# Attention into a token-and-channel mixer: the key maximum's broadcast and the key-value product moved beside h1, with the broadcast multiplied by the identity

## Chip, cores and metric

The kernel runs on one core of one Trainium2 chip. The metric is the device time of one execution in microseconds (us). Before the change it is 837.05 us, the median of 3 runs (833.13 to 837.97).

## What is computed

For 8 samples with 8 heads of 576 positions by 64 channels, both softmaxes (of q along its channels, of k along the positions) feed a linear attention, and its output `x` (576 x 512 for each sample) goes through a mixer along the positions and one along the channels. Cut to what matters:

```python
q_s = softmax(q, axis=-1)          # maximum taken off, exp, sum + 1e-9
k_s = softmax(k, axis=2)           # along the positions
kv  = einsum('bhsd,bhse->bhde', k_s, v)
x   = einsum('bhsd,bhde->bhse', q_s, kv)         # as (b, 576, 512)
h   = relu(x.T @ w_tok1) @ w_tok2                # along the positions, 576 -> 256 -> 576
u   = x + h.T
out = u + relu(u @ w_ch1) @ w_ch2                # along the channels, 512 -> 1536 -> 512
```

The weights come as float64 and are brought to float32 on the chip.

## The kernel before, in words

A *unit* is one pair of heads of one sample: 128 channels by 576 positions (five blocks of 128, the last one half filled). There are 32 units, four to a sample (j = 0 to 3). Units 0 to 7 ("early") are worked off ahead of the large loop, units 8 to 31 ("late") inside it.

A unit's stages, with the lines of the profile:

- `load_unit` (L123) issues the loads of kt (L128), q (L131) and, for late units, k (L135) on the SP queue; `load_v` (L141) those of v (L145, L146). For late units there is one buffer for kt and one for v, and there are two each for q and k.
- `softmax_k` (L205): VectorE takes the maximum `mc` of each channel from kt, which has the channels on its partitions (L208). k has them along its free dimension, so for a late unit the maximum has to be laid along the free dimension on all partitions: ScalarE writes the identity scaled by `mc` into `dg` (L223), TensorE multiplies a tile of ones by it (L225, "the broadcast" below), ScalarE copies the result to `mb` (L227), GpSimd subtracts it from k (L228), ScalarE takes the exponential (L229).
- `softmax_q` (L231): VectorE and ScalarE (L236 to L242); for a late unit q is then split into a high part `qh` (ScalarE) and a low part `ql` (GpSimd, both L105/L106), as are nearly all operands of the large products.
- `stage_qT` (L278): VectorE turns q in blocks of 32 (L297), 16 copies on VectorE and ScalarE put the blocks in place (L305), and q is split again into `qth`, `qtl`.
- `stage_kv` (L252): ten matmuls (L259, two column tiles of 64, one for each head; 20 records, since an unsplit float32 matmul is recorded as two), VectorE's reciprocal of the sum (L264, L265), ScalarE's scaling into `kvf` (L269), the split into `kvh`, `kvl`.
- `stage_y` (L308): 14 split matmuls of 256 columns (L319) and a copy `ys` (L321).
- `stage_h1` (L324): two unsplit matmuls of 128 columns (L327, four records), then `hh` on ScalarE (L334) and `hl` on VectorE (L335).
- `stage_u` (L346), two halves: nine split matmuls each (L364), of `kvh`/`kvl` with `qth`/`qtl` and of `hh`/`hl` with w_tok2, then a split of the result into the slot `uT` (L371, L372).

The large loop has 108 steps: 9 groups g of 512 positions by 12 blocks f. A step is `ch1(g, f)` (L385: 12 split matmuls of 512 columns, L393, then `h2h` on ScalarE L396 and `h2l` on VectorE L397) and then `ch2` (L401, 12 matmuls of 512 columns, L406) of the step before it. At the end of a group `out_end` (L423) adds the residual to the four accumulators (L430) and issues the output's DMAs; `residual` (L414) computes that residual ahead on GpSimd (L419) into staging tiles, which the output's DMAs of the group before must have left.

The work of the late units is put between: the dictionary `todo` holds functions for the place after ch1 of step i (key i) and after ch2 of step i (key i + 0.5). For a unit of the samples 3 to 7, whose steps start at `n0 + (b - 3) * 12`, n0 = 24:

```python
at = [n0 + (b - 3) * NF + 3 * j + x for x in (0, 1, 1.5, 2)]
...
put(at[0], s1)                          # stage_qT, stage_kv of unit n
put(at[0], lambda n=n: soft(n + 1))     # softmax_k, softmax_q of unit n + 1
put(at[0] + 0.5, lambda n=n: begin(n + 2))
```

and then stage_y at the second place, stage_h1 and the first half of stage_u together at the third, the other half at the fourth. So the unit with j = 0 has stage_kv and the next unit's broadcast in the first step of a group.

This order is not the engines' order yet. A planner in the framework simulates the program with costs of its own and, on each engine, takes among the instructions that its simulation has ready the one that stands first in the program. An engine's queue then runs in the order so found. All small products of the units and ch1 share four PSUM banks (`ps_h`); ch2's accumulators hold the other four.

Of the kernel before, what the change touches and what calls it, by code (L numbers as in the profile page):

```python
# [8 lines left out]
F32 = mybir.dt.float32  # L9
F32R = mybir.dt.float32r  # L10
U32 = mybir.dt.uint32
AF = mybir.ActivationFunctionType
ALU = mybir.AluOpType
AX = mybir.AxisListType

P = 128
# [4 lines left out]
def attn_mixer_kernel(ctx: ExitStack, tc: tile.TileContext, q, k, kt, v, wt, out, dims):  # L21
# [3 lines left out]
    nc = tc.nc  # L25
    B, H, S, D, TOK, DM, DCH, wide = dims
    NJ = DM // P
    NF = DCH // P
    NT = TOK // P
    C = S // P  # L30
    C1 = C + 1
    S0 = C * P
    TL = S - S0
    NG = B * S // CW
    NU = B * NJ
    NE = 2 * NJ
    F_HEAD, F_MORE = 4, 8

    const = ctx.enter_context(tc.tile_pool(name="const", bufs=1))
# [3 lines left out]
    sm = ctx.enter_context(tc.tile_pool(name="sm", bufs=2))  # L43
# [7 lines left out]
    ident = const.tile([P, P], F32R, name="ident")  # L51
# [3 lines left out]
    def v_tile(pool):  # L55
        t = pool.tile([P, C1, 2, D + 1], F32, name="v_t")
        nc.gpsimd.memset(t[:, :, :, D : D + 1], 1.0)
        nc.gpsimd.memset(t[TL:P, C, :, :], 0.0)
        return t

    v_ring = [v_tile(const)]

    ones = const.tile([P, P], F32, name="ones")
    nc.gpsimd.memset(ones, 1.0)


    ebias = const.tile([P, 1], F32, name="ebias")
    nc.gpsimd.memset(ebias, -(896.0 + 20.0) * 2.0**23)
# [1 line left out]
    def kv_tile(pool, i):  # L70

        t = pool.tile([P, P], F32, name=f"kvf{i}")
        nc.gpsimd.memset(t, 0.0)
        return t

    kv_ring = [kv_tile(const, 0)]

    w1h = const.tile([P, C, TOK], F32R, name="w1h")
    w1l = const.tile([P, C, TOK], F32R, name="w1l")
# [20 lines left out]
    def f32(ap):  # L100
        return ap.bitcast(F32)

    def split(hi, lo, src, lo_eng):

        nc.scalar.copy(hi, src)  # L105
        lo_eng.tensor_tensor(lo, src, f32(hi), op=ALU.subtract)  # L106
# [3 lines left out]
    def ps_unit(dtype=F32):  # L110

        pools = unit_banks[0]
        pool, name = pools[turn[0] % len(pools)]
        turn[0] += 1
        return pool.tile([P, 512], dtype, name=name)
# [25 lines left out]
    def load_v(n):  # L141
        if n < NU and n not in v_of:
            t = v_ring[n % 2 if n < NE else 0]
            for h in range(2):
                nc.sync.dma_start(t[:, 0:C, h, 0:D], v[n][:, 0:C, h * D : (h + 1) * D])  # L145
            nc.sync.dma_start(t[0:TL, C, :, 0:D], v[n][0:TL, C, :].rearrange("p (h d) -> p h d", h=2))  # L146
            v_of[n] = t
# [54 lines left out]
        split(*c2[f], load_weights(AT_C2 + f), nc.vector)  # L202


    def softmax_k(u):  # L205
        ktt = u["kt"]
        mc = sm.tile([P, 1], F32, name="mc")
        nc.vector.tensor_reduce(mc, ktt, axis=AX.X, op=ALU.max)  # L208
        kx = u["k"]
        if u["early"]:  # L210
            nc.vector.tensor_scalar(mc, mc, -1.0, None, op0=ALU.mult)
            nc.scalar.activation(ktt, ktt, AF.Exp, bias=mc)
            t = ps_unit()
            for c in range(C):
                nc.tensor.transpose(t[:, c * P : (c + 1) * P], ktt[:, c * P : (c + 1) * P], f32(ident))
            nc.scalar.copy(kx[:, 0:C, :], t.rearrange("p (c d) -> p c d", c=C))
            t = ps_unit()
            nc.tensor.transpose(t[:, 0:P], ktt[:, S0 : S0 + P], f32(ident))
            nc.scalar.copy(kx[:, C, :], t[:, 0:P])
            return  # L220

        dg = sm.tile([P, P], F32, name="dg", bufs=1)
        nc.scalar.activation(dg, f32(ident), AF.Copy, scale=mc)  # L223
        t = ps_unit()
        nc.tensor.matmul(t[:, 0:P], ones, dg, start=True, stop=True)  # L225
        mb = sm.tile([P, P], F32, name="mb", bufs=1)
        nc.scalar.copy(mb, t[:, 0:P])  # L227
        nc.gpsimd.tensor_tensor(kx, kx, mb.unsqueeze(1).broadcast_to([P, C1, P]), op=ALU.subtract)  # L228
        nc.scalar.activation(kx, kx, AF.Exp)  # L229
# [22 lines left out]
    def stage_kv(u):  # L252
        kx, vt = u["k"], v_of[u["n"]]
        kv = ps_unit()

        for c in range(C1):
            for h in range(2):
                hs = slice(h * D, (h + 1) * D)
                nc.tensor.matmul(kv[hs, 0 : D + 1], kx[:, c, hs], vt[:, c, h, :], start=(c == 0), stop=(c == C))  # L259

        if u["n"] != NE - 1:
            load_v(u["n"] + 2 if u["n"] < NE else u["n"] + 1)
        rs = sm.tile([P, 1], F32, name="rs")
        nc.vector.tensor_scalar(rs, kv[:, D : D + 1], 1e-9, None, op0=ALU.add)  # L264
        nc.vector.reciprocal(rs, rs)  # L265
        kvf = kv_ring[u["n"] % len(kv_ring)]
        for h in range(2):
            hs = slice(h * D, (h + 1) * D)
            nc.scalar.activation(kvf[hs, hs], kv[hs, 0:D], AF.Copy, scale=rs[hs])  # L269
        u["kvf"] = kvf  # L270
        if u["early"]:
            return
        kvh = wk.tile([P, P], F32R, name="kvh")
        kvl = wk.tile([P, P], F32R, name="kvl")
        split(kvh, kvl, kvf, nc.vector)
        u["kvh"], u["kvl"] = kvh, kvl
# [68 lines left out]
    def stage_u(u, half):  # L345
        b, j = u["b"], u["j"]  # L346
        edge = (b + 1) * CW - b * S
        cut = min(max(edge, S - 320), 320)
        n0, n1 = ((0, cut), (cut, S))[half]
        N = n1 - n0  # L350
        ns = slice(n0, n1)
        t = ps_unit()
        if u["early"]:
            mm = [(u["kvf"], u["qt"][:, ns])]
        else:
            mm = [(u["kvh"], u["qth"][:, ns]), (u["kvh"], u["qtl"][:, ns]), (u["kvl"], u["qth"][:, ns])]
        for n in range(NT):
            mm += [
                (u["hh"][:, n, :], w2h[:, n, ns]),
                (u["hh"][:, n, :], w2l[:, n, ns]),  # L360
                (u["hl"][:, n, :], w2h[:, n, ns]),
            ]
        for i, (a, w) in enumerate(mm):
            nc.tensor.matmul(t[:, 0:N], a, w, start=(i == 0), stop=(i == len(mm) - 1))  # L364
        for g, a0, a1 in ((b, n0, min(n1, edge)), (b + 1, max(n0, edge), n1)):
            if a0 < a1:
                at = b * S + a0 - g * CW
                uh, ul = (x[:, j, at : at + a1 - a0] for x in uT[g])
                src = t[:, a0 - n0 : a1 - n0]
                emptied[:] = [  # L370
                    nc.scalar.copy(uh, src).ins,  # L371
                    nc.vector.tensor_tensor(ul, src, f32(uh), op=ALU.subtract).ins,  # L372
                ]
# [68 lines left out]
    units = {}  # L442

    def begin(n):
        if n < NU and n not in units:
            units[n] = load_unit(n // NJ, n % NJ)

    def soft(n):
        if n < NU:
            softmax_k(units[n])  # L450
            softmax_q(units[n])

    def pe_stages(n):
        def s1():
            stage_qT(units[n])
            stage_kv(units[n])

        def s2():
            stage_y(units[n])

        def s3():
            stage_h1(units[n])
            stage_u(units[n], 0)

        def s4():
            stage_u(units[n], 1)

        return s1, s2, s3, s4


    NB = 3
    early_pools = ExitStack()
    early = early_pools.enter_context(tc.tile_pool(name="early", bufs=NB))
    early1 = early_pools.enter_context(tc.tile_pool(name="early1", bufs=1))
# [2 lines left out]
    w1f = early1.tile([P, C1, TOK], F32, name="w1f")  # L477
    w1t = early1.tile([P, TOK], F32, name="w1t")
    v_ring.append(v_tile(early1))
    kv_ring += [kv_tile(early1, i) for i in range(1, NB)]  # L480


    stages = [pe_stages(n) for n in range(NE)]
# [22 lines left out]
            with behind(emptied):  # L506
                split_tok1()
    early_pools.close()
    del v_ring[1:], kv_ring[1:]
    ld = ctx.enter_context(tc.tile_pool(name="ld", bufs=2))  # L510
    wk = ctx.enter_context(tc.tile_pool(name="wk", bufs=1))
    c2_rows(F_HEAD, F_MORE)
# [8 lines left out]
    n0 = len(steps)  # L521
    steps += [(g, f) for g in range(2, NG) for f in range(NF)]

    todo = {}

    def prepare():
        begin(NE)
        begin(NE + 1)
        soft(NE)

    def put(at, fn):
        todo.setdefault(int(2 * at) / 2, []).append(fn)

    put(n0 - 12, prepare)
    for n in range(NE, NU):
        b, j = divmod(n, NJ)
        if b == 2:
            at = (n0 - 10, n0 - 9, n0 - 9, n0 - 7.5) if j == 0 else [n0 - 9.5 + 2 * j + x for x in (0, 0.5, 1, 1.5)]
        else:
            at = [n0 + (b - 3) * NF + 3 * j + x for x in (0, 1, 1.5, 2)]  # L540
        s1, s2, s3, s4 = pe_stages(n)
        put(at[0], s1)
        put(at[0], lambda n=n: soft(n + 1))
        put(at[0] + 0.5, lambda n=n: begin(n + 2))
        for x, fn in zip(at[1:], (s2, s3, s4)):
            put(x, fn)

    pend = None

# [84 lines left out]
```

## Time and profile before

| what | before |
|---|---|
| median of 3 runs | 837.05 us |
| runs | 837.05, 833.13, 837.97 us |
| profiled execution | 836.64 us, of which its span (first to last instruction) is 834.8 us |
| mean granted TensorE clock | 0.994 |
| instructions | 11727 |
| busy | TensorE 807.8 us (97%), VectorE 492.6 us (59%), ScalarE 321.2 us (38%), GpSimd 113.3 us (14%) |
| DMA | 63.54 MB, mean 76 GB/s |

In a view of groups a row is: line, engine, operation, output<-inputs, shapes, count | busy us, mean ns of one | idle time before them and who ended it. In a timeline a row is: start in us, length in us, engine, line, operation, output<-inputs, shapes, count, and in brackets the idle time just before it with who ended it. The lengths of matmuls overlap, because they are pipelined; the distance between two starts is what a matmul costs in a stream.

### The profile page before, as it was taken

What the parts mean: (1) busy time and instruction counts of PE and PEld (TensorE: products, weight loads), DVE (VectorE), ACT (ScalarE), POOL (GpSimd) and SP (SyncE); (2) the same over time, 40 slices, a digit from 0 to 9 for tenths busy, and PEclk for the clock granted to TensorE, in tenths of its full rate; (3) what the DMA queues carried; (4) which work ended last, traced back from release to release, by engine and by line L of the source; (5) the groups of instructions that cost most, each with busy time, mean ns of one, the idle gap of its engine ahead of it and who ended that gap; (6) DMA issues with size and microseconds to landing.
All of it is one profiled execution on the core that took longest, in us unless ns stands there. A gap on an engine that the chain in (4) does not pass through costs nothing.

```text
span 834.8 us, 11727 instructions
## 1 busy us (share of the span) xinstructions
PE 807.8 (97%) x4464; PEld 673.8 (81%) x4464; DVE 492.6 (59%) x1088; ACT 321.2 (38%) x746; POOL 113.3 (14%) x93
## 2 busy tenths in 40 slices
PE   3899999989999999999999999999999999999997
PEld 3788888778888888788888888888888888888885
DVE  7999989899775555755556555755565323112111
ACT  4676443455544334433434433434443321101110
POOL 1000000112211011311122011311131102002000
PEclk9999999999999999999999999999999999999999
DMA  8653532424222122322232221312121001001001
GB/s 272 184 165 108 190 130 84 131 75 135 76 66 79 54 54 62 97 62 62 62 113 62 62 62 42 95 54 62 42 85 47 15 1 51 1 0 51 1 1 51
DMA packets 60632, 63.54 MB, mean 76 GB/s; under 512 B 40864, under 2 KB 40992, under 8 KB 60576
## 3 DMA queue, kind: packets, MB, share of 16 engines
q1 hardware_dynamic: 55392, 53.36, 21.9%
q10 hardware_dynamic: 5184, 9.44, 3.0%
q8 instruction: 35, 0.57, 0.3%
q14 instruction: 21, 0.17, 0.1%
HBM read 53.35 MB, written 9.44 MB: 75 GB/s over the span
## 4 chain that ended last, share of the span: by engine, by line
PE 79%; DVE 12%; DMA 4%; issue 2%; ACT 1%; POOL 1%; SPq 0%; DVEq 0%; POOLq 0%; ACTq 0%
PE ps_h L393 31%; PE ps_o L406 31%; PE ps_h L364 6%; PE ps_h L319 4%; DVE q_t L305 3%; PE ps_h L259 2%; DMA out<-stg 2%; DMA q_t<-in_q 1%; PE ps_h L327 1%; PE ps_o L364 1%; PE ps_h L225 1%; DVE q_t L237 1%; DMA stg<-in_w 1%; DVE st L236 1%; POOL ql L106 1%
## 5 line engine op out<-in xcount | busy, mean ns | idle before, releaser
L397 DVE SCALAR_TENSOR_TENSOR h2l<-ps_h,h2h 128x512 fp32r<-128x512 f32 x108 | 74.1, 686 | 173.6 <-ACT h2h L396 173.6
L393 PE MATMUL ps_h<-uh,c1h 128*128 128x512 f32 x432 | 171.8, 398 | 0.0
L393 PE MATMUL ps_h<-ul,c1h 128*128 128x512 f32 x432 | 171.5, 397 | 0.0
L393 PE MATMUL ps_h<-uh,c1l 128*128 128x512 f32 x432 | 171.3, 396 | 0.0
L406 PE MATMUL ps_o<-h2h,c2l 128*128 128x512 f32 x432 | 169.1, 392 | 0.0
L406 PE MATMUL ps_o<-h2h,c2h 128*128 128x512 f32 x432 | 168.4, 394 | 0.2 <-ACT h2h L396 0.2
L396 ACT ACTIVATE h2h<-ps_h 128x512 fp32r<-128x512 f32 x108 | 64.4, 596 | 261.8 <-PE ps_h L393 255.7
L406 PE MATMUL ps_o<-h2l,c2h 128*128 128x512 f32 x432 | 152.4, 396 | 0.0
L305 DVE COPY q_t<-cv_s 32x160 f32<-32x160 f32 (+1 forms) x264 | 71.7, 272 | 62.5 <-POOL ql L106 59.2
L393 PEld LDWEIGHTS ps_h<-ul,c1h 128*128 128x128 f32 x432 | 81.8, 189 | 19.4
L393 PEld LDWEIGHTS ps_h<-uh,c1l 128*128 128x128 f32 x432 | 81.7, 189 | 17.0
L393 PEld LDWEIGHTS ps_h<-uh,c1h 128*128 128x128 f32 x432 | 81.6, 189 | 17.1
L406 PEld LDWEIGHTS ps_o<-h2h,c2h 128*128 128x128 f32 x432 | 81.1, 188 | 17.3 <-ACT h2h L396 0.4
L406 PEld LDWEIGHTS ps_o<-h2h,c2l 128*128 128x128 f32 x432 | 81.2, 188 | 16.9
L406 PEld LDWEIGHTS ps_o<-h2l,c2h 128*128 128x128 f32 x432 | 79.6, 188 | 16.3
L228 POOL TENSOR_TENSOR k_t<-k_t,mb 128x640 f32<-128x640 f32 x24 | 37.7, 1572 | 324.6 <-ACT mb L227 324.6
L106 POOL TENSOR_TENSOR ql<-q_t,qh 128x640 fp32r<-128x640 f32 x24 | 38.2, 1592 | 189.5 <-DMA stg<-in_w 100.7
L419 POOL TENSOR_TENSOR stg<-uh,ul 128x512 f32<-128x512 f32 x28 | 35.5, 1290 | 144.5 <-DMA out<-stg 86.8
L236 DVE TENSOR_REDUCE st<-q_t 128x10 f32<-128x640 f32 x32 | 26.1, 817 | 37.2 <-DMA q_t<-in_q 37.2
L238 ACT ACTIVATE q_t<-q_t 128x640 f32<-128x640 f32 x32 | 23.7, 741 | 45.3 <-DVE q_t L237 45.1
L305 ACT COPY q_t<-cv_s 32x128 f32<-32x128 f32 (+1 forms) x120 | 36.8, 307 | 2.2 <-DVE cv_s L297 0.8
L364 PE MATMUL ps_h<-w2h,hh 128*128 128x256 f32 (+1 forms) x112 | 32.9, 301 | 0.0
(143 smaller groups left out, 1150.4 us busy)
## 6 DMA issues: line engine op xcount, KB each, us to landing
stg<-in_w SPq DMA_DIRECT2D x28, 512.0 KB, 4.1
kt_t<-in_kt SPq DMA_DIRECT2D x32, 320.0 KB, 3.4
q_t<-in_q SPq DMA_DIRECT2D x32, 320.0 KB, 3.0
v_t<-in_v SPq DMA_DIRECT2D x64, 128.0 KB, 2.9
out<-stg ACTq DMA_DIRECT2D x32, 256.0 KB, 2.8
k_t<-in_k SPq DMA_DIRECT2D x24, 320.0 KB, 3.6
v_t<-in_v SPq DMA_DIRECT2D x32, 32.0 KB, 3.1
out<-part ACTq DMA_DIRECT2D x4, 256.0 KB, 2.7
```

What stands on the lines that cost most here:

```text
L106: lo_eng.tensor_tensor(lo, src, f32(hi), op=ALU.subtract)
L228: nc.gpsimd.tensor_tensor(kx, kx, mb.unsqueeze(1).broadcast_to([P, C1, P]), op=ALU.subtract)
L236: nc.vector.tensor_reduce(st[:, 0, :], qt, axis=AX.X, op=ALU.max)
L238: nc.scalar.activation(qc, qc, AF.Exp)
L305: eng(qx[ys, 0:n, xs], turned[xs, 0:n, ys])
L319: nc.tensor.matmul(y[:, 0:TOK], a, w, start=(i == 0), stop=(i == len(mm) - 1))
L364: nc.tensor.matmul(t[:, 0:N], a, w, start=(i == 0), stop=(i == len(mm) - 1))
L393: nc.tensor.matmul(t, a[:, f, n, :], w, start=(i == 0), stop=(i == 3 * NJ - 1))
L396: nc.scalar.activation(hh, t, AF.Relu).ins,
L397: nc.vector.scalar_tensor_tensor(hl, t, 0.0, f32(hh), op0=ALU.max, op1=ALU.subtract).ins,
L406: nc.tensor.matmul(o, a[:, cs], w, start=(first and i == 0), stop=(last and i == 2))
L419: nc.gpsimd.tensor_tensor(res[n], f32(uh), f32(ul), op=ALU.add)
```

## The change

The late units' stages are no longer kept together by unit. `softmax_k` is divided into `k_max` (the maximum) and `exp_k` (broadcast, subtraction, exponential); `stage_kv` loses its last lines to `split_kv`. In the broadcast the stationary operand is now the maximum itself, read with a stride of zero, and the moving one the identity; `dg` and `ones` are gone. Two of the three small tiles `kvf` live for the whole kernel instead of one, so that kv of a unit can be written while the unit before still has its own.

```diff
-    ones = const.tile([P, P], F32, name="ones")
-    nc.gpsimd.memset(ones, 1.0)
...
-    kv_ring = [kv_tile(const, 0)]
+    kv_ring = [kv_tile(const, i) for i in range(2)]
...
+    def exp_k(u):
+
         kx = u["k"]
...
-        dg = sm.tile([P, P], F32, name="dg", bufs=1)
-        nc.scalar.activation(dg, f32(ident), AF.Copy, scale=mc)
         t = ps_unit()
-        nc.tensor.matmul(t[:, 0:P], ones, dg, start=True, stop=True)
+        nc.tensor.matmul(t[:, 0:P], u["mc"].broadcast_to([P, P]), f32(ident), start=True, stop=True)
...
-    kv_ring += [kv_tile(early1, i) for i in range(1, NB)]
+    kv_ring.append(kv_tile(early1, 2))
...
-    del v_ring[1:], kv_ring[1:]
+    del v_ring[1:], kv_ring[2:]
...
+    at = [n0 - 8.5 + 2 * j for j in range(NJ)]
+    at += [n0 + (b - 3) * NF + 3 * j + 1 for b in range(3, B) for j in range(NJ)]
+    load(10, NE)
+    load(10, NE + 1)
+    put(11, k_max, NE)
+    put(11, exp_k, NE)
+    put(11, softmax_q, NE)
+    put(13, k_max, NE + 1)
+    put(13.5, exp_k, NE + 1)
+    put(13.5, stage_kv, NE)
+    put(14, split_kv, NE)
+    put(14, stage_qT, NE)
+    put(15, stage_y, NE)
+    put(15, softmax_q, NE + 1)
+    for i, a in enumerate(at):
+        n = NE + i
+        load(a - 1, n + 2)
+        put(a - 0.5, k_max, n + 2)
+        put(a, stage_h1, n)
+        put(a, exp_k, n + 2)
+        put(a, stage_kv, n + 1)
+        put(a + 0.5, lambda u: stage_u(u, 0), n)
+        put(a + 1, lambda u: stage_u(u, 1), n)
+        put(a + 1, split_kv, n + 1)
+        put(a + 1, stage_qT, n + 1)
+        if n + 1 < NU:
+            put(at[i + 1] - (1 if at[i + 1] - a > 2 else 0.5), stage_y, n + 1)
+            put(at[i + 1] - (1 if at[i + 1] - a > 2 else 0.5), softmax_q, n + 2)
```

So at a place `a` (steps 1, 4, 7 and 10 of a group, from sample 3 on) there stand h1 of unit n, the broadcast of unit n + 2 and kv of unit n + 1; the halves of stage_u follow half a step and a whole step later, stage_y stands a whole step ahead of h1 instead of half a step.

More of the change, by code (lines that the diff above doesn't have):

```diff
@@ L202, in load_ch, with k_max @@
         split(*c2[f], load_weights(AT_C2 + f), nc.vector)
+    def k_max(u):
+        mc = sm.tile([P, 1], F32, name="mc")
+        nc.vector.tensor_reduce(mc, u["kt"], axis=AX.X, op=ALU.max)
+        u["mc"] = mc
     def softmax_k(u):
-        ktt = u["kt"]
-        mc = sm.tile([P, 1], F32, name="mc")
-        nc.vector.tensor_reduce(mc, ktt, axis=AX.X, op=ALU.max)
-        kx = u["k"]
[L210 to L220, printed above, removed]
-        dg = sm.tile([P, P], F32, name="dg", bufs=1)
-        nc.scalar.activation(dg, f32(ident), AF.Copy, scale=mc)
+        k_max(u)
+        ktt, mc, kx = u["kt"], u["mc"], u["k"]
+        nc.vector.tensor_scalar(mc, mc, -1.0, None, op0=ALU.mult)
+        nc.scalar.activation(ktt, ktt, AF.Exp, bias=mc)
+        t = ps_unit()
+        for c in range(C):
+            nc.tensor.transpose(t[:, c * P : (c + 1) * P], ktt[:, c * P : (c + 1) * P], f32(ident))
+        nc.scalar.copy(kx[:, 0:C, :], t.rearrange("p (c d) -> p c d", c=C))
+        t = ps_unit()
+        nc.tensor.transpose(t[:, 0:P], ktt[:, S0 : S0 + P], f32(ident))
+        nc.scalar.copy(kx[:, C, :], t[:, 0:P])
+    def exp_k(u):
+        kx = u["k"]
         t = ps_unit()
-        nc.tensor.matmul(t[:, 0:P], ones, dg, start=True, stop=True)
+        nc.tensor.matmul(t[:, 0:P], u["mc"].broadcast_to([P, P]), f32(ident), start=True, stop=True)
         mb = sm.tile([P, P], F32, name="mb", bufs=1)
@@ L266, in stage_kv @@
         kvf = kv_ring[u["n"] % len(kv_ring)]
+        u["kvf"] = kvf
         for h in range(2):
@@ L269, in stage_kv, with split_kv @@
             nc.scalar.activation(kvf[hs, hs], kv[hs, 0:D], AF.Copy, scale=rs[hs])
-        u["kvf"] = kvf
-        if u["early"]:
-            return
+    def split_kv(u):
+        kvf = u["kvf"]
         kvh = wk.tile([P, P], F32R, name="kvh")
@@ L524, in attn_mixer_kernel, with put, load @@
     todo = {}
[L526 to L546, printed above, removed]
+    def put(at, fn, n):
+        if n < NU:
+            todo.setdefault(int(2 * at) / 2, []).append(lambda: fn(units[n]))
+    def load(at, n):
+        if n < NU:
+            todo.setdefault(int(2 * at) / 2, []).append(lambda: begin(n))
+    at = [n0 - 8.5 + 2 * j for j in range(NJ)]
[26 more added lines that the diff above has]
+            put(at[i + 1] - (1 if at[i + 1] - a > 2 else 0.5), softmax_q, n + 2)
     pend = None
```

## The prediction

> **What bounds the kernel now.** I read the page first: busy time by engine, then the chain that ended last; then the busy time by stretch; then the waits of TensorE (PE); then PE's timeline at the places that the change touches.
>
> ```profile
> PE 807.8 (97%) x4464; PEld 673.8 (81%) x4464; DVE 492.6 (59%) x1088; ACT 321.2 (38%) x746; POOL 113.3 (14%) x93
> ...
> PE 79%; DVE 12%; DMA 4%; issue 2%; ACT 1%; POOL 1%; SPq 0%; DVEq 0%; POOLq 0%; ACTq 0%
> ```
> ```profile
> 140.00:240.00 100.00, 97.52 (x545) 81.75 (x544) 86.93 (x186) 49.77 (x115) 19.37 (x13) 0.98 0.31 95
> 240.00:690.00 450.00, 447.80 (x2585) 375.50 (x2584) 251.45 (x582) 178.09 (x434) 79.54 (x54) 1.00 0.21 61
> ```
>
> From 240 to 690 us, where 20 of the 24 late units are worked off, PE is busy 447.8 of 450 us. VectorE (DVE) has nearly half its time free there, ScalarE (ACT) and GpSimd (POOL) more. After 690 no unit is left and nothing of the change reaches. From 140 to 240 DVE is at 87 of 100 us and close to being the bound. So time is won in one way only: PE has to do less, or wait less. "Busy" hides part of that, as records of matmuls overlap; what a piece costs PE is read from the distance between starts. The waits that the profile names for PE in the stretches touched are few, one at the start of the late units (its row stands below) and four of this kind:
>
> ```profile
> PE ps_h L364 <- DVE hl L335: 2.2, 4, 0.9
> ```
>
> **The change part by part.**
>
> *Standing together.* The words of the change suggest that small unsplit matmuls are dear because each interrupts the stream of split ones. What does such an interruption cost? First h1 and the broadcast alone:
>
> ```profile
> 171.74 0.39 PE L406 MATMUL ps_o<-h2l,c2h 128*128 128x512 f32 x1
> 171.97 0.60 PE L327 MATMUL ps_h<-kvf,ys 128*128 128x128 f32 x4
> ```
> ```profile
> 204.12 0.39 PE L406 MATMUL ps_o<-h2h,c2l 128*128 128x512 f32 x1
> 204.35 0.38 PE L225 MATMUL ps_h<-dg,ones 128*128 128x128 f32 x2
> 204.49 1.18 PE L406 MATMUL ps_o<-h2l,c2h 128*128 128x512 f32 x4
> 205.50 0.40 PE L393 MATMUL ps_h<-uh,c1h 128*128 128x512 f32 x1
> ```
>
> Both start 0.23 us after a matmul of 512 columns, which is the distance of two such matmuls in the stream: going in costs nothing. The stretch from 204.12 to 205.50 holds five of 512 columns, 1.15 us, so the broadcast costs 1.38 - 1.15 = 0.23 us for two records of 128 columns, its plain work. These two pay no toll, and there is none to save by putting them beside others. kv is another matter (its matmuls use 64 columns of the array, 128*64 in the rows). Whole, with the broadcast behind it:
>
> ```profile
> 539.42 0.40 PE L406 MATMUL ps_o<-h2h,c2l 128*128 128x512 f32 x1
> 539.75 0.80 PE L259 MATMUL ps_h<-v_t,k_t 128*64 128x65 f32 x20
> 540.48 0.49 PE L225 MATMUL ps_h<-dg,ones 128*128 128x128 f32 x2
> 540.73 0.70 PE L406 MATMUL ps_o<-h2l,c2h 128*128 128x512 f32 x2
> 541.27 0.40 PE L406 MATMUL ps_o<-h2h,c2h 128*128 128x512 f32 x1
> ```
>
> 1.85 us with three of 512 columns in it: 1.85 - 0.69 = 1.16 us, of which the broadcast is 0.23 and kv 0.93. kv starts 0.33 us after its predecessor, 0.10 later than the stream would, and the two behind it are late as well. kv still goes in once and comes out once when h1 and the broadcast stand ahead of it, so a whole group costs what its parts cost now. **Term 1: 0.** Bounds: nothing, and all of kv's entry of 0.10 us for 23 units, 2.3 us, if the unsplit neighbour spared it; I take nothing, since 128*128 neighbours are what it has now.
>
> *kv no longer cut up.* At four starts of a group (near 334, 426, 516 and 607 us) the planner has put kv between matmuls of ch1; a piece of the first, and the whole third, are:
>
> ```profile
> 334.90 0.33 PE L259 MATMUL ps_h<-v_t,k_t 128*64 128x65 f32 x2
> ...
> 515.61 0.40 PE L406 MATMUL ps_o<-h2h,c2h 128*128 128x512 f32 x1
> 515.94 0.33 PE L259 MATMUL ps_h<-v_t,k_t 128*64 128x65 f32 x2
> 516.20 0.50 PE L393 MATMUL ps_h<-uh,c1h 128*128 128x512 f32 x1
> 516.53 0.39 PE L393 MATMUL ps_h<-uh,c1l 128*128 128x512 f32 x1
> 516.85 0.33 PE L259 MATMUL ps_h<-v_t,k_t 128*64 128x65 f32 x2
> 517.11 0.49 PE L393 MATMUL ps_h<-ul,c1h 128*128 128x512 f32 x1
> 517.53 0.69 PE L259 MATMUL ps_h<-v_t,k_t 128*64 128x65 f32 x16
> 518.15 0.49 PE L225 MATMUL ps_h<-dg,ones 128*128 128x128 f32 x2
> 518.39 0.94 PE L406 MATMUL ps_o<-h2l,c2h 128*128 128x512 f32 x3
> 519.17 0.40 PE L406 MATMUL ps_o<-h2h,c2l 128*128 128x512 f32 x1
> ```
>
> From 515.61 to 519.17 are 3.56 us with seven matmuls of 512 columns, 1.62 us: kv and broadcast cost 1.94 instead of 1.16, so 0.78 for two extra pieces. The cause can be read in the order: in the first step of a group the last three matmuls of ch1 need the slot of the unit just finished (uh, ul); where the planner's simulation has them late, it fills with kv's first pair, goes back, and so on. After the change the first step of a group holds stage_y and no kv; kv stands in steps 1, 4, 7 and 10; in the steps 3, 6 and 9 of the kernel before, as far inside a group, none was cut from 240 us on. **Term 2: 4 x 0.78 = 3.1 us less.** Bounds: 0 (cut elsewhere) and 3.1.
>
> [...]
>
> *h1 half a step ahead of stage_u.* Now h1 and the first half of stage_u have one place, and `hl` (ACT's hh, then DVE) is needed some 4 us later. At the first unit of a group that isn't enough:
>
> ```profile
> 529.58 0.60 PE L327 MATMUL ps_h<-kvf,ys 128*128 128x128 f32 x4
> ...
> 533.83 0.32 PE L364 MATMUL ps_h<-w2h,hh 128*128 128x320 f32 x1
> 533.98 0.30 PE L364 MATMUL ps_h<-w2l,hh 128*128 128x320 f32 x1
> 534.75 0.39 PE L364 MATMUL ps_h<-w2h,hl 128*128 128x256 f32 x1 [0.47 <-DVE hl L335]
> ```
> ```profile
> 529.47 4.78 DVE L305 COPY q_t<-cv_s 32x160 f32<-32x160 f32 x11 [3.79 <-POOL ql L106]
> 534.28 0.42 DVE L335 SCALAR_TENSOR_TENSOR hl<-ps_h,hh 128x256 fp32r<-128x256 f32 x1
> ```
> ```profile
> 525.38 2.53 POOL L419 TENSOR_TENSOR stg<-uh,ul 128x512 f32<-128x512 f32 x2 [4.79 <-DMA out<-stg]
> 527.87 1.56 POOL L106 TENSOR_TENSOR ql<-q_t,qh 128x640 fp32r<-128x640 f32 x1
> ```
>
> This is one chain, read upwards: `hl` stands in DVE's queue behind the copies of the next unit's q; these wait for that unit's `ql` on POOL; and `ql` stands in POOL's queue behind the residual, which waits for the output's DMA. PE starts 0.77 us after the matmul before instead of 0.15: 0.62 lost, where the wait shows 0.47. So the four waits, 2.2 us together, cost 2.2 + 4 x 0.15 = 2.8. After the change stage_y of the first unit moves to the group's first step, ahead of ch2; `qh` of the next unit, whose buffer waits only for that stage_y, is then written before the output's DMAs are even issued, `ql` goes through POOL ahead of the residual, and the chain dissolves. Besides, between h1 and its use now lie broadcast, kv (1.2 us) and twelve matmuls of ch2 (2.8 us), which hide hh and hl. **Term 3: 2.8 us less.** Bounds: 2.8 less, and the loss that the last rival works out.
>
> *The start, units 8 and 9.*
>
> ```profile
> 174.82 0.41 PE L364 MATMUL ps_h<-qth,kvh 128*128 128x320 f32 x1 [2.24 <-ACT qth L105]
> ```
> ```profile
> 175.00:180.00 5.00, 5.00 (x18) 4.06 (x18) 4.82 (x15) 3.51 (x10) 0.00 (x0) 0.66 0.23 66
> ```
>
> The first late stage_u waits 2.2 us for the turned q, and behind the wait the granted clock is 0.66 over 5 us, which costs (1 - 0.66) x 5 = 1.7 us more. The change loads these units two steps earlier, takes their softmax a step earlier and puts stage_u of unit 8 a step later. It could win both, 3.9 us. But DVE has no room between 170 and 210 us, the copies are the same, and whatever PE gains it may wait out for DVE a little later. Bounds 0 and 3.9; nearer to nothing, as DVE's 4.82 busy of these 5 us says. **Term 4: 1.2 us less.** [...]
>
> *What costs nothing.* The identity as the moving operand: two records of 128 columns as before. With a stride of zero the load of the stationary operand is not shown by any row. The nearest, and what leaves ACT, are:
>
> ```profile
> L225 PEld LDWEIGHTS ps_h<-dg,ones x48: 186/188/190, 148.8 to 653.3; 128*128 128x128 f32 x48
> ```
> ```profile
> L223 ACT ACTIVATE dg<-ident,mc 128x128 f32<-128x128 f32 x24 | 9.7, 405 | 0.0
> ```
>
> The load is hidden under the matmul before. Bounds: no change, and all 48 loads of 0.19 us laid bare, 9 us more; I take no change, as the load only reads its numbers from another place. `dg` frees 9.7 us of ACT, which is idle for 60% of the time. PE's queue now holds the broadcast right behind h1 and ahead of kv, so a late `mc` would hold up kv and ch2; but kt's load waits only for the maximum of the unit before, three steps earlier. The loads keep their number; on the SP queue kt, q and k of a unit now go ahead of its v, which is needed two or more steps later. `kvh` of a unit waits in ACT's queue for the first half-products of the unit before, with `h2h` behind it; that place is the one in which the simulation sees both ready.
>
> *The sum*, against the profiled execution: 836.64 - 0 - 3.1 - 2.8 - 1.2 = 829.5 us. That execution is 0.4 us under the median shown and the runs lie 4.8 us apart, so I make no correction: **829.5 us**, 0.9% less.
>
> **The rivals.**
>
> *The start is won whole.* For it: stage_u of unit 8 gets half a step of ch2 as cover. Against it: DVE. Then 3.9 instead of 1.2, and up to 0.9 for kv of the units 8 and 9, which are cut once each (half of 0.78 each): 826 us.
>
> *Nothing is won.* The place in the program isn't the place on PE: the planner may part the three, cut kv anew, or find other late operands, since what makes it cut is a simulated wait. For it: its simulation did that four times. Against it: never at the steps 3, 6 and 9 from 240 us on. Time: 836.6.
>
> *Slower: the first unit of a group waits for hl.* h1 and stage_u move forward against the group's start, the chain over the output's DMA does not. Were DVE's order to stay as it is, hl would be there at 534.7 on the old scale. It would be wanted after ch1, stage_y, ch2, ch1, the three together, ch2 and the first of stage_u: 2.8 + 1.6 + 2.8 + 2.8 + 1.6 + 2.8 + 0.9 = 15.3 us into the group (stage_y as 14 matmuls of half the columns, six of stage_u at 0.15), against 534.1 - 512.1 = 22.0 now:
>
> ```profile
> 512.13 0.39 PE L393 MATMUL ps_h<-uh,c1h 128*128 128x512 f32 x1
> ```
>
> So 6.7 us more than the 0.6 of now, at four groups 27 us: 836.64 - 3.1 - 1.2 + 27 = 859. It decides from 3.3 us more a group on (13 us for four: 845.4). For it: the planner did put the copies ahead of hl. Against it: the moved stage_y, which lets `ql` go first.
>
> **How the numbers follow.** About 1% (8.4 us) is what a measurement of this kernel can tell from no change. Forecast 0.55 (826.5 to 833), start won whole 0.17 (826), nothing won 0.16 (834 to 840), slower 0.12. Faster by over 1%, under 828.7: a third of the first and nearly all of the second, 0.36. Slower by over 1%: the last and a sliver of the third, 0.13. Within 1%: 0.51. The range: from all terms at their best, 836.6 - 3.1 - 2.8 - 3.9 - 0.9 = 826, less a little for the spread of runs, 825; up to nothing won at the upper runs of before, 838.
>
> **What would show it.** Right: 24 pieces of kv from 160 us on but for the first two units, each 20 records long, no wait for hl at PE, `ql` ahead of the residual on POOL. h1, broadcast and kv cost 1.6 us together, as apart. Wrong: a group much under 1.6 us (term 1), kv in pieces (term 2), a wait at L364 that has moved (term 3), DVE busy throughout from 165 to 210 with new waits at ch2 (term 4).

## The result and the profile after

| | runs | median us | lowest to highest | profiled execution (span) |
|---|---|---|---|---|
| before | 6 | 836.06 | 833.13 to 837.97 | 836.64 (834.8) |
| after | 6 | 847.81 | 845.23 to 849.70 | 846.0 (844.2) |

The ratio is 1.0139 [1.0122, 1.0157]: the kernel became slower by 1.4%. The forecast was 829.5 us, with a range from 825 to 838. The mean granted clock is 0.994 in both profiled executions.

The page of after, as for before: busy time by engine, the chain that ended last, and one group, the copies that put the turned q in place. Behind it that group in the page of before.

```profile
PE 804.6 (95%) x4464; PEld 674.9 (80%) x4464; DVE 524.1 (62%) x1088; ACT 309.4 (37%) x722; POOL 116.1 (14%) x92
...
PE 76%; DVE 17%; DMA 3%; issue 2%; ACT 1%; SPq 0%; DVEq 0%; ACTq 0%
...
L306 DVE COPY q_t<-cv_s 32x160 f32<-32x160 f32 (+1 forms) x264 | 95.7, 362 | 8.7 <-POOL ql L103 5.4
```
```profile
L305 DVE COPY q_t<-cv_s 32x160 f32<-32x160 f32 (+1 forms) x264 | 71.7, 272 | 62.5 <-POOL ql L106 59.2
```

TensorE (PE) has no more to do than before. VectorE (DVE) is busy for 31.5 us more with the same 1088 instructions, and 24.0 of these are the 264 copies: the same work, 362 ns each instead of 272. DVE's share of the chain rises from 12% to 17%.

The busy time by stretch of after (columns: stretch, length, then busy us and count of PE, weight loads, DVE, ACT, POOL, then granted clock, DMA share, GB/s):

```profile
140.00:240.00 100.00, 93.43 (x550) 77.75 (x550) 86.47 (x181) 46.43 (x109) 20.18 (x13) 1.00 0.35 101
240.00:690.00 450.00, 439.19 (x2538) 372.57 (x2538) 281.61 (x584) 168.08 (x416) 81.70 (x54) 1.00 0.21 61
```

From 240 to 690 us PE was busy for 447.8 us and is now for 439.2; DVE went from 251 to 282. The waits of PE in these stretches, from the view of waits (total us, times, longest):

```profile
PE ps_h L394 <- DVE h2l L398: 10.8, 4, 3.1
...
PE ps_h L365 <- DVE hl L336: 3.0, 2, 1.8
PE ps_o L407 <- ACT h2h L397: 2.6, 2, 2.1
```

The first is new, once at each start of a group (PE goes on at 353, 445, 538 and 630 us). The other two belong to the units 8 to 11. The four waits for `hl` at the group starts of before are gone. Kv is one piece of 20 records for all 24 late units. Around the third of the new waits PE's timeline has:

```profile
528.47 0.40 PE L394 MATMUL ps_h<-ul,c1h 128*128 128x512 f32 x1
528.70 0.61 PE L328 MATMUL ps_h<-kvf,ys 128*128 128x128 f32 x4
529.15 0.39 PE L225 MATMUL ps_h<-ident,mc 128*128 128x128 f32 x2
529.46 0.80 PE L259 MATMUL ps_h<-v_t,k_t 128*64 128x65 f32 x20
530.20 0.50 PE L407 MATMUL ps_o<-h2h,c2h 128*128 128x512 f32 x1
530.53 0.40 PE L407 MATMUL ps_o<-h2h,c2l 128*128 128x512 f32 x1
...
534.33 0.40 PE L407 MATMUL ps_o<-h2h,c2l 128*128 128x512 f32 x1
537.85 0.51 PE L394 MATMUL ps_h<-uh,c1h 128*128 128x512 f32 x1 [3.12 <-DVE h2l L398]
```

h1, the broadcast and kv stand together. From 528.47 to 530.53 are 2.06 us with two matmuls of 512 columns (0.46) in them, so the three cost 1.60. Then comes the loss: from 534.33 to 537.85 are 3.52 us, where 0.23 would be the plain distance. The four such places have 3.02, 2.92, 3.52 and 2.94 us, 11.5 more than 4 x 0.23.

What held `h2l` stands in DVE's queue at that place, and beside it what POOL did:

```profile
528.35 7.99 DVE L306 COPY q_t<-cv_s 32x160 f32<-32x160 f32 x11
536.37 0.84 DVE L298 STREAM_TRANSPOSE cv_s<-q_t 128x640 f32<-128x640 f32 x1
537.14 0.65 DVE L398 SCALAR_TENSOR_TENSOR h2l<-ps_h,h2h 128x512 fp32r<-128x512 f32 x1
...
538.43 0.41 DVE L336 SCALAR_TENSOR_TENSOR hl<-ps_h,hh 128x256 fp32r<-128x256 f32 x1
```
```profile
524.97 1.58 POOL L103 TENSOR_TENSOR ql<-q_t,qh 128x640 fp32r<-128x640 f32 x1 [15.71 <-ACT qh L102]
528.54 2.51 POOL L420 TENSOR_TENSOR stg<-uh,ul 128x512 f32<-128x512 f32 x2 [1.99 <-DVE stg L431]
531.01 1.57 POOL L228 TENSOR_TENSOR k_t<-k_t,mb 128x640 f32<-128x640 f32 x1
532.54 2.53 POOL L420 TENSOR_TENSOR stg<-uh,ul 128x512 f32<-128x512 f32 x2
```

`ql` (524.97) does go through POOL ahead of the residual (L420), as predicted. So the copies of q start early, and now at the same moment as the residual and the subtraction of the maximum (L228). The eleven copies take 7.99 us. `h2l` stands behind them in the queue, though `h2h`, its other input, was there at 529.50; the PSUM bank that it reads stays taken, and the next ch1 has none.

Where the time goes along the run (us by which after is behind before when the last ch2 matmul of the step starts, both counted from the start of the span):

| step | 11 | 24 | 36 | 48 | 60 | 72 | 105 |
|---|---|---|---|---|---|---|---|
| after | +0.3 | +4.7 | +4.0 | +5.1 | +6.2 | +8.1 | +9.0 |

At step 24 after has already done unit 12's kv and unit 13's broadcast, 1.16 us that before does later; so the start loses 3.5 us. With the forecast's terms 2 and 3 as gains: 836.64 + 3.5 + 11.5 - 3.1 - 2.8 = 845.7, against 846.0.

### The profile page after: what moved, and what is told of

Read it like the earlier page. It is cut to its first block, busy times and chain, and to the rows that moved or that the text cites. A ratio compares the mean times of both kernels' runs of the same rounds, so it can differ in the third digit from the quotient of the medians.

```text
span 844.2 us, 11799 instructions
## 1 busy us (share of the span) xinstructions
PE 804.6 (95%) x4464; PEld 674.9 (80%) x4464; DVE 524.1 (62%) x1088; ACT 309.4 (37%) x722; POOL 116.1 (14%) x92
## 4 chain that ended last, share of the span: by engine, by line
PE 76%; DVE 17%; DMA 3%; issue 2%; ACT 1%; SPq 0%; DVEq 0%; ACTq 0%
PE ps_h L394 30%; PE ps_o L407 28%; PE ps_h L365 7%; DVE q_t L306 6%; PE ps_h L320 5%; DMA stg<-in_w 2%; PE ps_h L259 2%; DMA q_t<-in_q 1%; PE ps_o L365 1%; PE ps_h L328 1%; DVE stg L431 1%; DVE st L239 1%; DVE q_t L242 1%; DVE h2l L398 1%; PE ps_o L320 1%
## 5 line engine op out<-in xcount | busy, mean ns | idle before, releaser
L394 PE MATMUL ps_h<-uh,c1h 128*128 128x512 f32 x432 | 171.9, 398 | 11.7 <-DVE h2l L398 10.8
L407 PE MATMUL ps_o<-h2h,c2h 128*128 128x512 f32 x432 | 170.9, 398 | 2.7 <-ACT h2h L397 2.6
L398 DVE SCALAR_TENSOR_TENSOR h2l<-ps_h,h2h 128x512 fp32r<-128x512 f32 x108 | 74.2, 687 | 148.0 <-ACT h2h L397 146.8
L407 PE MATMUL ps_o<-h2l,c2h 128*128 128x512 f32 x432 | 161.6, 393 | 0.0
L394 PEld LDWEIGHTS ps_h<-uh,c1h 128*128 128x128 f32 x432 | 81.2, 188 | 31.5 <-DVE h2l L398 12.6
L306 DVE COPY q_t<-cv_s 32x160 f32<-32x160 f32 (+1 forms) x264 | 95.7, 362 | 8.7 <-POOL ql L103 5.4
L103 POOL TENSOR_TENSOR ql<-q_t,qh 128x640 fp32r<-128x640 f32 x24 | 40.4, 1685 | 407.4 <-ACT qh L102 391.0
L373 DVE TENSOR_TENSOR ul<-ps_h,uh 128x320 fp32r<-128x320 f32 (+4 forms) x76 | 28.6, 376 | 67.9 <-ACT uh L372 67.8
L420 POOL TENSOR_TENSOR stg<-uh,ul 128x512 f32<-128x512 f32 x28 | 35.5, 1288 | 147.4 <-DMA out<-stg 110.2
L228 POOL TENSOR_TENSOR k_t<-k_t,mb 128x640 f32<-128x640 f32 x24 | 38.6, 1607 | 109.9 <-ACT mb L227 109.9
L372 ACT CAST uh<-ps_h 128x320 fp32r<-128x320 f32 (+4 forms) x76 | 25.5, 335 | 49.8 <-PE ps_h L365 40.3
```

What stands on the lines that cost most here:

```text
L306: eng(qx[ys, 0:n, xs], turned[xs, 0:n, ys])
L394: nc.tensor.matmul(t, a[:, f, n, :], w, start=(i == 0), stop=(i == 3 * NJ - 1))
L398: nc.vector.scalar_tensor_tensor(hl, t, 0.0, f32(hh), op0=ALU.max, op1=ALU.subtract).ins,
L407: nc.tensor.matmul(o, a[:, cs], w, start=(first and i == 0), stop=(last and i == 2))
L420: nc.gpsimd.tensor_tensor(res[n], f32(uh), f32(ul), op=ALU.add)
```

## The experiments

**Theory:** the whole loss at the group starts is the meeting of copies and residual, with `h2l` behind the slowed copies; the start is a second loss with a cause of its own, its new spacing. **Rivals:** the order on DVE alone (copies ahead of `h2l`, at whatever speed); the grouping on PE, with the PSUM banks that it holds; the identity as operand. `behind(x)` in the code keeps the planner from putting what stands in it ahead of the instructions x on their engine. Each median is followed by lowest and highest, and by the ratio to runs of before taken beside it (their medians are 836.0 to 836.7 us).

### Moving the residual away from the copies

`pool_ops` holds the subtractions L228 in order of the program; the residual is put behind one of the next sample.

```diff
-            residual(g)
+            with behind(pool_ops[-3 : len(pool_ops) - 2]):
+                residual(g)
```

> The changed kernel with one difference: on GpSimd the residual (four subtractions' worth of adds, L420) is ordered behind the subtraction of the group's fifth step instead of the group's first steps. The order on TensorE, VectorE, ScalarE and SP stays as in the changed kernel. Theory 1 (the copies of the turned q on VectorE and GpSimd's residual cannot run at once, so 11 copies take 8.0 us instead of 2.7 at each group's start, and h2l behind them is late): copies back to about 2.7 us, the four waits of ch1 for h2l (10.8 us) gone, 836 to 839 us. Theory 2 (it is the order on VectorE alone: 11 copies and a turn ahead of h2l): waits and time stay, 846 to 849 us. Theory 3 (h1, broadcast and kv hold three of the four PSUM banks at once, and ch1 finds none): as theory 2.

Measured: 840.94 us (837.31 to 843.79, 10 runs), 1.0049 [1.0029, 1.007], 2 us above the 836 to 839 that were expected. PE, DVE, ACT and SP have the order that they have in after; only POOL's differs. The waits of PE, DVE at the third group start and POOL there:

```profile
PE ps_h L394 <- DVE h2l L398: 2.6, 1, 2.6
```
```profile
522.32 3.99 DVE L306 COPY q_t<-cv_s 32x160 f32<-32x160 f32 x11
...
527.11 0.65 DVE L398 SCALAR_TENSOR_TENSOR h2l<-ps_h,h2h 128x512 fp32r<-128x512 f32 x1
```
```profile
523.92 1.61 POOL L228 TENSOR_TENSOR k_t<-k_t,mb 128x640 f32<-128x640 f32 x1 [3.41 <-PE ps_h L259]
...
547.61 5.04 POOL L420 TENSOR_TENSOR stg<-uh,ul 128x512 f32<-128x512 f32 x4
```

The same copies, in the same place of DVE's queue, take 3.99 instead of 7.99 us, and three of the four waits are gone. The fourth (PE goes on at 620 us) is at the one group start where residual and copies still met. So the order on DVE alone does not cost the time; the meeting does. Nor do the PSUM banks that h1, the broadcast and kv hold, the third theory: PE's order is that of after.

A second form puts the residual behind the subtraction of the next sample's last unit (`pool_ops` goes by units here):

```diff
-            residual(g)
+            with behind([pool_ops[min(NU - 1, NJ * (g + 1) + 3)]]):
+                residual(g)
```

> As the run with the late residual, but for every group it is ordered behind the subtraction of that group's own fourth unit, so that also the last group with units is covered, where the earlier run kept a wait of 2.6 us. The order on TensorE, VectorE, ScalarE and SP is again that of the changed kernel. Theory 1 (copies against GpSimd): no wait of ch1 for h2l is left, no copy over 0.5 us at the five group starts, 2 to 3 us under the earlier run, 837 to 839 us as the median. Theory 2 (order on VectorE): the waits return, 846 us.

Measured: 836.27 us (832.60 to 839.03, 10 runs), 0.9993 [0.9971, 1.0015]. That is a little under the 837 to 839 expected, though not every wait is gone: one of 2.4 us is left, and it makes its own test. There the planner put the two together again; DVE and POOL at that place:

```profile
455.80 6.97 DVE L306 COPY q_t<-cv_s 32x160 f32<-32x160 f32 x11
462.80 0.69 DVE L398 SCALAR_TENSOR_TENSOR h2l<-ps_h,h2h 128x512 fp32r<-128x512 f32 x1
```
```profile
457.37 1.61 POOL L228 TENSOR_TENSOR k_t<-k_t,mb 128x640 f32<-128x640 f32 x1 [3.05 <-ACT mb L227]
458.94 4.97 POOL L420 TENSOR_TENSOR stg<-uh,ul 128x512 f32<-128x512 f32 x4
```

### Moving the copies behind h2l instead

`drained` holds `h2h` and `h2l` of the step.

```diff
+    def turn_behind(u):
+        with behind(drained):
+            stage_qT(u)
...
-        put(a + 1, stage_qT, n + 1)
+        put(a + 1, turn_behind, n + 1)
```

> The changed kernel with stage_qT ordered on VectorE and ScalarE behind the h2h and h2l of the step in which it stands, so that the copies cannot be pulled ahead of h2l. Theory 1: the copies come after the residual, take 2.7 us, and no wait of ch1 for h2l is left; about 837 us, and something more lost or won at the start of the late units. Theory 2: the same, 837 us, even where copies and GpSimd still meet. Theory 3: h2l comes early and the banks are free early, so the waits fall too; this run parts none of the three, but shows whether the lost time is that of the place of the copies on VectorE. If it stays at 847 us, all three are wrong.

Measured: 836.91 us (835.27 to 837.98, 10 runs), 1.0001 [0.9988, 1.0015]. It is 8.0 us behind before at step 24 and 0.3 at step 105: the late part wins 7.7, all of it lost at the start. The mean copy is back at 248 ns.

### The start alone as before

Units 8 to 11 are placed by the table of before; the rest as in after.

```diff
...
+        p = (n0 - 10, n0 - 9, n0 - 9, n0 - 7.5) if j == 0 else [n0 - 9.5 + 2 * j + x for x in (0, 0.5, 1, 1.5)]
+        put(p[0], stage_qT, n)
+        put(p[0], stage_kv, n)
...
+        put(p[1], stage_y, n)
+        put(p[2], stage_h1, n)
+        put(p[2], lambda u: stage_u(u, 0), n)
+        put(p[3], lambda u: stage_u(u, 1), n)
...
```

> The changed kernel, but units 8 to 11 (sample 2) keep the places of the kernel before; from unit 12 on the new order. If the 4.7 us by which the changed kernel is behind at step 24 come from the new places of these four units: 843 us, level with the kernel before at step 24. If they come from the new order as such (the steps behind would lose them instead) or from the identity: 847 us.

Measured: 846.22 us (843.55 to 849.25, 4 runs), 1.0107 [1.0072, 1.0142]. From step 11 to 24 it loses 1.2 us instead of 4.3, which is the 1.16 done earlier: no loss at the start. The four waits stay (10.8 us). It missed its forecast of 843 because the group starts cost it more: from step 24 to 105 its profiled execution (847.97 us) loses 8.7 us where after loses 4.3. One of them, PE's timeline and the stretch behind it:

```profile
536.87 0.50 PE L394 MATMUL ps_h<-uh,c1h 128*128 128x512 f32 x1 [3.11 <-DVE h2l L398]
```
```profile
537.00:545.00 8.00, 8.00 (x34) 6.80 (x35) 3.73 (x10) 2.95 (x8) 0.00 (x0) 0.79 0.15 43
```

The clock of 0.79 over 8 us is 1.7 us lost; from 342 to 352 us, around the first of its four waits, it is 0.93, and from 240 to 690 us 0.99, some 4.5 us by that rounded figure, where after has 1.00 (also in the 8 us behind each of its four waits). The two fastest of its four executions took 843.55 and 844.47 us, near the forecast, at granted clocks of 0.994 and 0.996; the other two, 847.97 and 849.25 us, have 0.990 and 0.986. Such drops probably also widen the spread of the other kernels that have these waits (an estimate: the six executions of after have clocks from 0.987 to 0.994); only one execution of each has a trace.

### Both together

> Two of the runs put together: units 8 to 11 at the places of the kernel before, and from unit 12 on the new order with stage_qT ordered behind the h2h and h2l of its step. If the changed kernel is late for two separate reasons (its start, 3 us; its group starts, 11 us of waits) and its two gains (kv whole 3.1 us, hl in time 2.8 us) are real: 829 to 832 us, faster than before. If the gains were not real or the reasons overlap: 836 us.

Measured: **829.90 us** (829.24 to 830.10, 4 runs), 0.9921 [0.9906, 0.9936]. The stretches, then DVE at the third group start:

```profile
140.00:240.00 100.00, 96.53 (x564) 80.69 (x563) 84.53 (x179) 48.43 (x113) 21.76 (x14) 1.00 0.34 101
240.00:690.00 450.00, 449.99 (x2599) 382.88 (x2599) 252.05 (x591) 172.08 (x417) 82.53 (x53) 1.00 0.21 61
```
```profile
522.61 0.68 DVE L398 SCALAR_TENSOR_TENSOR h2l<-ps_h,h2h 128x512 fp32r<-128x512 f32 x1
...
530.98 2.71 DVE L306 COPY q_t<-cv_s 32x160 f32<-32x160 f32 x11
```

PE is busy for 449.99 of 450 us, and the eleven copies take 2.71 us with no POOL instruction beside them. Against before it stands at +0.2 us at step 24 and at -7.2 at step 105. Of these 7.4 us, 1.2 is the work done earlier, and 6.2 is left where the terms 2 and 3 said 5.9.

With the residual moved instead of the copies (the edit of the second form above, on the old start):

> Units 8 to 11 at the places of the kernel before, the new order from unit 12 on, and the residual late on GpSimd; VectorE's order as the planner has it. Under theory 1 the two losses are gone without touching VectorE's order: 829 to 833 us. Under theory 2 the waits at the group starts stay: 843 us or more.

Measured: 833.75 us (829.74 to 834.64, 6 runs), 0.9961 [0.9943, 0.998]. One wait for `h2l` of 2.6 us at 458 us is left, again where the two met.

### The rivals on PE

The three apart, on the 829.90 kernel:

```diff
-        put(a, exp_k, n + 2)
-        put(a, stage_kv, n + 1)
+        put(a + 0.5, exp_k, n + 2)
...
+        put(a + 1, stage_kv, n + 1)
```

> As the run that joins the old start with the turn behind h2l, but from unit 11 on h1, the broadcast and kv no longer stand together on TensorE: h1 stays, the broadcast stands half a step later, kv a whole step. If standing together is worth nothing by itself (h1 and the broadcast enter a stream of 512-column matmuls without a toll, kv pays its own either way): within 1.5 us of that run, with about 1.6 us for the three pieces of a unit, as together. If it is worth one toll per unit (0.1 to 0.4 us by 20 units): 2 to 8 us slower than that run.

Measured: 830.18 us (829.54 to 830.66, 4 runs), 0.9925 [0.9911, 0.994], beside 829.90 for the same kernel with the three together. On PE the broadcast and kv do stand apart from h1 there from unit 12 on. The title's grouping is worth nothing that shows.

The identity alone, on the kernel before:

```diff
-        dg = sm.tile([P, P], F32, name="dg", bufs=1)
-        nc.scalar.activation(dg, f32(ident), AF.Copy, scale=mc)
-        nc.tensor.matmul(t[:, 0:P], ones, dg, start=True, stop=True)
+        nc.tensor.matmul(t[:, 0:P], mc.broadcast_to([P, P]), f32(ident), start=True, stop=True)
```

> The kernel before with only the broadcast changed: maximum with stride zero as the stationary operand, identity as the moving one, no dg and no ones; kvf tiles and places as before. If the identity costs nothing: 836 us, within 2. If the load of the stationary operand with stride zero were slow and bare: up to 9 us more, 845 us, with two records of the broadcast taking more than 0.23 us together.

Measured: 837.60 us (836.62 to 839.89, 10 runs), 1.0019 [1.0004, 1.0034], 1.6 us more. The planner's order shifts with the missing ACT instruction, so these 1.6 us can't be put down to the operand. The traces speak for the order: between two matmuls of 512 columns the broadcast starts 0.23 us after the first and the second 0.14 us after the broadcast's start, in before (at 204.35 us) as in after with the identity as operand (at 143.81 and 152.60 us), while the waits for `hl` at the group starts have grown by 2.0 us, from 2.2 to:

```profile
PE ps_h L364 <- DVE hl L335: 4.2, 3, 2.0
```

### The chain in the kernel before

The edit of the second form, on the kernel before:

> The kernel before with only GpSimd's order changed: the residual behind the subtraction of the group's fourth unit; the order on TensorE, VectorE, ScalarE and SP is that of the kernel before. It tests the prediction's third term by itself: that hl is late at a group's start because the copies wait for ql, and ql for the residual. If so, no copy of the turned q over 1 us at the group starts, the four waits for hl (2.2 us) and no more gone: 833 to 834 us. If hl is late for another reason: 836 us with the waits in place.

Measured: 833.29 us (832.12 to 836.16, 10 runs), 0.9966 [0.9953, 0.998], 3.1 us less. PE's waits and DVE at the third group start:

```profile
PE ps_h L364 <- DVE hl L335: 0.5, 1, 0.5
```
```profile
524.31 2.72 DVE L305 COPY q_t<-cv_s 32x160 f32<-32x160 f32 x11 [1.10 <-POOL ql L106]
```

The four waits for `hl` at the group starts, 2.2 us, are gone (the 0.5 us are at 181 us, in the start), and the copies, 4.78 us in the forecast's row, take 2.72. The chain that the forecast read for term 3 is confirmed, but it held a second delay besides the late `ql`: two us of slowed copies.

### The start

Two more on the 829.90 kernel or its like. First, h1 and the first half of stage_u of the units 8 to 11 half a step later, in the old spacing:

```diff
-        put(p[2], stage_h1, n)
-        put(p[2], lambda u: stage_u(u, 0), n)
+        put(p[2] + 0.5, stage_h1, n)
+        put(p[2] + 0.5, lambda u: stage_u(u, 0), n)
```

> The joined kernel (old start, turn behind h2l) with one more change: h1 and the first half of stage_u of unit 8 half a step later, behind twelve matmuls of ch2. The joined kernel's longest wait in the late part is h1's for ys, 2.1 us. If that wait is paid for in full: 828 us. If VectorE sets the pace there and the wait only moves: 830 us.

Measured: 829.80 us (829.63 to 831.06, 4 runs), 0.9925 [0.9905, 0.9945]: nothing beside 829.90. The wait for `ys` that it was to remove is 1.9 us long and still there. Second, the new spacing with stage_u of the units 8 to 11 half a step later, and the copies behind `h2l` from unit 13 on (the recorded expectation says 12; with `i >= NJ` the first turn put behind is that of unit 13):

```diff
+        x = 0.5 if i < NJ else 0
+        put(a + 0.5 + x, lambda u: stage_u(u, 0), n)
+        put(a + 1 + x, lambda u: stage_u(u, 1), n)
...
+        put(a + 1, turn_behind if i >= NJ else stage_qT, n + 1)
```

> New places for all units, the turn behind h2l from unit 12 on (as in the joined kernel), and for units 8 to 11 both halves of stage_u half a step later than the changed kernel has them. If the start's loss of 3 us comes from hl that is wanted too early in the two-step spacing (two waits of 3.0 us together at L365): 830 us, level with the joined kernel. If it comes from something else at the start (h2h behind the turned q's split on ScalarE, kv(9) and h1(8) early): 832 to 834 us.

Measured: 829.97 us (829.20 to 831.07, 4 runs), 0.9924 [0.9904, 0.9945]. Its waits of PE at the start:

```profile
PE ps_o L407 <- ACT h2h L397: 3.1, 2, 2.1
...
PE ps_h L365 <- DVE hl L336: 1.0, 1, 1.0
```

The waits for `hl` fall from 3.0 to 1.0, and at step 24 it is 2.1 us behind before instead of 4.7, 0.9 without the work done earlier. So most of the start's loss, 2.6 of the 3.5 us, comes from wanting `hl` too soon, half a step behind h1 where units stand two steps apart.

## Why the forecast was wrong, point by point

- **Term 1 (the three together, 0): right.** 1.60 us for the three, and the kernel with the three apart takes the same time within 0.3 us.
- **Term 2 (kv no longer cut, -3.1) and term 3 (no wait for `hl`, -2.8): right as gains**, and in the trace of after: kv is whole at the group starts, and none of the old waits is left. Without the new losses they come to 6.2 us together, where 5.9 was said. The residual alone moved in the kernel before gives 3.1 for term 3; term 2 has no run of its own, and 3.1 is what is left for it.
- **The step that failed is in term 3: "`ql` goes through POOL ahead of the residual, and the chain dissolves".** The first half happened. The chain did not dissolve, it changed places. Copies freed early ran into the residual that had been ahead of them, took 8.0 us where they take 2.7 undisturbed (4.8 in before), and held up `h2l`, the operand of the large loop itself, instead of `hl`. The prediction asked what waits for the freed step, and not what it will now run beside. Price: +11.5 us.
- **The row to see it by was quoted.** The forecast shows eleven copies of 4.78 us at 529.47, with POOL's `ql` ahead of them, and takes them as given. Eleven at the row's usual speed are 2.6 us (254 of the 264 copies in before run beside no POOL instruction and take 0.235 us each). What slowed these was there to be found: the other 10 overlap one, and the nine of them that began after it had begun took 1.24 to 1.48 us.
- **Term 4 (the start, -1.2) had the wrong sign: +3.5.** The old wait is still there in another form, and `hl` is late besides; PE, then DVE, then POOL:

```profile
176.26 1.19 PE L407 MATMUL ps_o<-h2h,c2h 128*128 128x512 f32 x4 [2.11 <-ACT h2h L397]
...
219.81 0.41 PE L365 MATMUL ps_h<-w2h,hl 128*128 128x320 f32 x1 [1.77 <-DVE hl L336]
```
```profile
213.59 4.00 DVE L306 COPY q_t<-cv_s 32x160 f32<-32x160 f32 x11
...
219.34 0.42 DVE L336 SCALAR_TENSOR_TENSOR hl<-ps_h,hh 128x256 fp32r<-128x256 f32 x1
```
```profile
215.17 1.63 POOL L228 TENSOR_TENSOR k_t<-k_t,mb 128x640 f32<-128x640 f32 x1 [4.09 <-ACT mb L227]
```

  The first is the 2.24 us of before one place on: the same late copies, now with `h2h` behind `qth` in ACT's queue. The waits there come to 6.5 us (3.0, 2.6, and 0.9 for `kvf` and `mb`) against 2.24 and 1.7 of clock before; that makes 2.6 of the 3.5; of the other 0.9, 0.3 is there already at step 11, and the rest is not itemised. The wait of before was itself in good part the same collision: ahead of `qth` one copy, begun inside `ql` on POOL, took 1.48 us instead of 0.22 (1.54 in after). That is about 1.3 of the 2.24 us, an estimate from these two lengths; no run takes it away alone. The forecast had named this sign of error, DVE full and new waits at ch2.
- **The slower rival named the right place and the wrong victim.** It had the planner's copies ahead of a late product on DVE, but for `hl`, and it was set low because of "the moved stage_y, which lets `ql` go first". That argument was true, and it was the cause.
- **The identity costs nothing: held** within 1.6 us of 837, far from the bound of 9.

With both losses removed, the change reaches 829.8 to 830.2 us in four kernels, 0.8% less than before, where the forecast had 829.5. That they come so near is in part luck: 829.5 counts 1.2 us for term 4, which was not won; terms 2 and 3 alone make 830.7. The faster kernel is thus the change with the copies kept behind `h2l` and the start either as before or with stage_u half a step later.

## What to carry to other kernels

When a step is freed from a chain, ask what it will now run beside on the other engines, and not only who waits for it. A row whose instructions take longer than the same ones elsewhere (4.78 us for eleven copies that take 2.7) was here a contention already at work; explain such a row before moving anything near it. And look who stands behind the moved instructions in their queue: here a delay there held the operand of the main loop and cost 11.5 us.

## What the runs showed of the hardware

**In the traces of before and after, a VectorE copy of q that begins inside a GpSimd instruction ends only after it.** In after 221 of the 264 copies of 32x160 or 32x128 float32 overlap no POOL instruction and take 0.234 us on average; 43 overlap one. Of these, 12 began 0.02 to 0.22 us ahead of it and took 0.22 to 0.25 us, as if it were not there. The other 31 began after it had begun, and each ended 0.08 to 0.12 us after it had ended, however late it began: 1.33 us on average, at most 1.64 (the POOL instructions take 1.29 us for a piece of the residual, 1.57 for `ql` and L228, all medians). In before 10 of the 264 overlap one: the one that began first took 0.22 us, the other nine ended 0.08 to 0.11 us after it. The residual and L228 touch no tile of the copies, so it is no dependency. Eleven copies take 2.71 us with no POOL instruction beside them (the 829.90 kernel), 3.99 with one (the first form of the late residual), 6.97 and 7.99 with five (its second form, and after). The residual is hardly longer for it: two of its instructions take 2.51 us beside the copies in after, and 2.53 in before at 525.38 us, where no copy runs. Other instructions are hit too: in after the last product of q's softmax (L242, 128x640) takes 0.83 us alone and 1.04 to 2.12, on average 1.70, in the 13 cases that begin inside a POOL instruction. The transpose (L298, 0.84 us), the maximum (L204, 0.81) and `h2l`, which reads one operand from PSUM (L398, 0.69), take as long there inside a POOL instruction as alone: 0.85, 0.81 and 0.69 us in 5, 8 and 9 cases. What in the chip makes the copies wait was not shown; the runs show the collision and its price.

**A wait of 2.1 to 3.1 us was in some cases followed by a lower clock, and in others not:** after 2.24 us in before (0.66 over 5 us) and after 3.11 us in the run with the old start (0.79 over 8 us), but after none of the four waits of 2.5 to 3.1 us in the profiled execution of after, nor after its wait of 2.11 us at 174 us (1.00 over the 8 us behind each). In before the clock is 0.50 from 175.93 to 179.34 us, 3.41 us long, and matmuls of 512 columns start 0.43 us apart there instead of 0.23; in the run with the old start they start 0.42 to 0.43 us apart from 538.84 to 541.39 us. Either drop cost 1.7 us beside the wait itself. No run was made for it, and what decides whether a drop follows was not shown.
